# A recurrent-memory transformer on one core: the second turn of the probabilities as row-tile products in four banks, value groups and late outputs spread evenly over the steps, x as bf16 rows, dense weights loaded earlier

## The chip, the cores and the metric

The kernel runs on one core of a Trainium2 chip. The metric is the device time of one execution in microseconds (us); lower is better. Of the engines, TensorE (PE; its weight loads are shown apart as PEld) does the matrix products, VectorE (DVE) and ScalarE (ACT) read the results out of PSUM and do elementwise work, GpSimd (POOL) does elementwise work on SBUF, and SyncE (SP) issues most transfers.

## The reference

Four stages in a row on x (2048 rows of 512): attention with a recurrent memory, a dense block, the same attention again, the same dense block, each on a layer-normalized input and added to its residual.

```python
def _A_ref(x, mem0, Wq, Wk, Wv, Wo, seg_len):      # H = 32 heads of 128, M = 8, seg_len = 32
    mem = mem0
    for s in range(n_seg):                         # 64 segments
        h = concatenate([mem, x[segment s]])       # 8 + 32 = 40 rows
        q, k, v = h @ Wq, h @ Wk, h @ Wv           # per head
        p = softmax(mask(q @ k.T * scale))
        o = (p @ v) @ Wo                           # summed over heads
        mem = o[:8]
        outs.append(o[8:])
def _B_ref(x, w1, w2):                             # 512 -> 1376 -> 512
    return relu(x @ w1) @ w2
x = x + _A_ref(_layernorm(x), ...)
x = x + _B_ref(_layernorm(x), ...)
x = x + _A_ref(_layernorm(x), ...)
x = x + _B_ref(_layernorm(x), ...)
```

The memory makes attention sequential: segment s + 1 needs the memory that segment s left.

## The kernel before, in words

Everything is bf16 with f32 sums; all weights stay in SBUF. The program is one straight line of 67 steps (`step(k)`, k = 0 to 66; step 0 is `first_step`). Step k does segment k of the first attention layer (a = 0) and segment k - 3 of the second (a = 1) side by side, and between their parts the dense block for the segments that are ready. Steps 3 to 63 have both layers; the first three and the last three have one and are called single.

Inside a step with both layers the order on TensorE, VectorE, SP and GpSimd is the order of the source (`manual_schedule`); only ScalarE's order is left to the scheduler, which `evict_behind` steers: an eviction marked `late` is issued behind the last exponential. A step runs:

- `qk(0)`: queries and keys of heads 0 to 15 (tile `qp`, 128 products of 80 columns), then a piece of filler work, then `scores` into two banks that are kept for scores (`sp_banks`), `exponentials`, `softmax(0)`. The first half of the probabilities (`P_sb`) is turned by a transposing transfer (`turn_p`, on SP).
- `qk(1)`: the same for heads 16 to 31, then `dense_h` (tile `hp`), the second `scores`, `softmax(1)`. Its result `P1_sb` (in the profile it too is named P_sb) comes partly from GpSimd and, for a = 1, from VectorE.
- While the softmax runs on VectorE and ScalarE, TensorE has filler: value groups (`vp`), the values of the next segment of layer 1 (`v`), the late outputs (`wox`) and the second dense product (`dense_y`, written into a scores bank, so it shows as sp<-w_sb,hT).
- The second half is then turned on TensorE (`transpose_p(1, 5)`, tile `tp`, line 623): 16 products of a 128 x 64 block with the two-block identity, 80 columns each, in column tiles, into two banks of the pool `ps_c`: five slots copied out by ScalarE, three by VectorE, into `PT_sb`. The last 8 products of `dense_y` (from `f_mid = 9` on) stand between the turn and what follows.
- `weighted_v`: 64 products (`pv`), two row tiles of 40 rows at a time, heads in three groups of 12, 12 and 8, each with its bank; `outputs` copies them into `OTm` (memory rows) and `OTx` (token rows), VectorE for a = 0 and ScalarE for a = 1.
- `output_mem` (tile `wo`), `output_own` (`own`), the new memory (`mt`) and its values (`vm`); then `prepare(k + 1)`, which adds to the residual and normalizes.

PSUM has eight banks: `ps_c` three, `sp_banks` two, `ps_wo` one, `ps_fill` two.

What the change touches:

- `load_x` (lines 115 to 118): the rows of x of a segment go by two GpSimd transfers, which widen them to f32, into the residual tile; `add_own` (400 to 405) adds the attention's own output to it.
- `load_dense` (154 to 158): w1, then w2 in two parts; called in step 1 from `probabilities` (line 902). In step 0 the space of w1 and w2 serves as staging for values.
- `values_at` (739 to 748): which value groups (8 products each, the values of 64 tokens) are due in step k. From step 5 to step 61 the odd steps have one or two groups, the even ones none.
- `output_late` (379 to 385) and `add_late` (387 to 393): for a segment of layer 1 whose output does not ride with the memory output (every second one), 64 products in the step behind it, 20 of them ahead of the first scores (`first = 10` heads), into the bank of `ps_wo`, and two additions on VectorE ahead of the turn's copies. So odd steps have groups and no late outputs, even steps late outputs and no groups.

The steps in one table (k = 5 to 62):

| steps | value groups | late products | called below |
|---|---|---|---|
| even | 0 | 64 | even step |
| odd, 10 of 29 | 1 | 0 | one-group step |
| odd, 19 of 29 | 2 | 0 | two-group step |

Of the kernel before, what the change touches and what calls it, by code (L numbers as in the profile page):

```python
# [22 lines left out]
def kernel(  # L23
# [90 lines left out]

    def load_x(k):
# [38 lines left out]
    def load_dense():  # L154
        nc.sync.dma_start(out=w1_sb[:], in_=B_w1.rearrange("(c p) f -> p c f", p=128))
# [41 lines left out]
    P1_sb = const.tile([128, 16 * L + 24], BF)  # L197
# [110 lines left out]
    def values0(p, n, lo=0, hi=NC4, pool=None, stage=None, late=False):  # L308
        r = 64 * (p % 2)
        if (n, lo) == (0, 0):  # L310
            vd0[p] = dram.tile([4, 2, 64, 512], BF, tag="vd0", bufs=4, name="vd0")
# [54 lines left out]
    def output_rows(t, a, lo, hi):  # L366

        for h in range(lo, hi):
            for j in range(2):
                q = 32 * (2 * (h % 2) + j)  # L370
                nc.tensor.matmul(t[q:q + 32, 0:HALF], lhsT=OTx[:, h, SEG * a:SEG * a + SEG],  # L371
                                 rhs=Wo_sb[:, h, HALF * j:HALF * j + HALF], start=(h < 2), stop=(h >= H - 2),
                                 tile_position=(0, q))

    def late_rows(k):
        s = k - 1
        return s if has1(s) and not ride1(s) else None

    def output_late(k, lo, hi):
        if late_rows(k) is None:  # L380
            return
        if lo == 0:
            pool, tag = (ps_wo, "wo") if k <= LAST else (ps_c, "c")
            wo_tiles[k] = pool.tile([128, Dm], F32, tag=tag, name="wox")
        output_rows(wo_tiles[k], 1, lo, hi)

    def add_late(k, parts=range(2)):
        if late_rows(k) is None:
            return
        d, o = place1(late_rows(k))  # L390
# [9 lines left out]
    def add_own(k):  # L400
# [3 lines left out]
        for part in range(2):  # L404
            nc.vector.tensor_tensor(out=R, in0=R, in1=own_tiles[k][64 * part:64 * part + 64, 0:HALF], op=ALU.add)
# [194 lines left out]
    def softmax(hf, act, by_pe=False, ess=None):  # L600
        if ess is None:
            ess = exponentials(act)
        if by_pe and hf:
            transpose_p(0)
        for a, es in ess.items():
# [4 lines left out]
            P = P1_sb[:, 0:16 * L].rearrange("p (s a q) -> p s a q", s=8, a=2)[:, :, a, :] if hf else \  # L610
                P_sb[:, :, 64 * a:64 * a + L]
            eng.tensor_tensor(out=P, in0=es[:],  # L612
                              in1=sm[:].unsqueeze(2).to_broadcast([128, 8, L]), op=ALU.mult)

    def transpose_p(hf, cut=4):

        for s0, ns, copy in ((0, cut, nc.scalar.copy), (cut, 8 - cut, nc.vector.tensor_copy)):
            tp = ps_c.tile([128, ns, 2, L], F32, tag="c", name="tp")
            for sl in range(ns):
                for a in range(2):  # L620
                    c = L * (2 * (s0 + sl) + a)
# [435 lines left out]
```

## Time and profile before

| | |
|---|---|
| time before, median of 3 runs | 1618.14 us (1617.14 to 1618.94) |
| the profiled execution | 1617.83 us |
| its span in the profile | 1616.0 us, 103053 instructions |
| VectorE, ScalarE, GpSimd busy | 76%, 45%, 23% of the span |
| granted TensorE clock, mean | 0.998 |
| transfers | 146.25 MB, 91 GB/s on the mean |

How to read it: a row of the timeline has the start in us from the span's start, the duration, the engine, the line, the operation, output<-inputs, shapes and count; in brackets is the idle time of the engine just before, and what ended it. Successive instructions of one kind are merged (x24), and consecutive rows of an engine can overlap, since products and copies are pipelined: the time that a group takes from its engine is the difference of the starts of its row and the next. In a table of stretches the columns are the stretch, its length, busy time (and count) of PE, PEld, DVE, ACT and POOL, the granted clock, the transfer engines' share and GB/s. In rows of groups, the figure behind the busy time is the mean of one in ns.

### The profile page before, as it was taken

To read this page: it belongs to the slowest core of one execution; us is meant where nothing else is said; L and a number is where in the kernel's file an instruction comes from. 1 tells how busy PE (TensorE), PEld (TensorE's weight loads), DVE (VectorE), ACT (ScalarE), POOL (GpSimd) and SP (SyncE) were. 2 spreads that over 40 slices of the span, in tenths; PEclk is the share of its full clock that TensorE was granted. 3 is DMA by queue.
4 is the path that set the end of the run, shared out by engine and by line. 5 is a ranking of instruction groups with operands and counts; after the bars stand their busy time and mean duration, and the time that the engine had idled before them with its cause. 6 is when DMAs were issued, how large, how long until landed. Compare 5 with 4: busy or idle time off the path is not lost.

```text
span 1616.0 us, 103053 instructions
## 1 busy us (share of the span) xinstructions
PE 1568.8 (97%) x46705; PEld 1273.1 (79%) x46706; DVE 1229.6 (76%) x3463; ACT 728.4 (45%) x1708; POOL 365.4 (23%) x733
## 2 busy tenths in 40 slices
PE   6899999999999999999999999999999999999997
PEld 3578878888878877887888887788788878878875
DVE  4477878777877877887777787778777777877765
ACT  3344444444444444444444444444444444444442
POOL 2022222122222222212222222222222222222210
PEclk9999999999999999999999999999999999999999
DMA  9734343434344444443433444353443334335321
GB/s 367 217 90 78 84 75 86 88 74 87 76 85 82 84 89 70 93 76 77 90 83 87 72 84 82 71 96 79 81 83 76 83 70 90 79 74 86 74 66 38
DMA packets 226757, 146.25 MB, mean 91 GB/s; under 512 B 124392, under 2 KB 222736, under 8 KB 226320
## 3 DMA queue, kind: packets, MB, share of 16 engines
q1 hardware_dynamic: 220080, 135.44, 38.7%
q0 software_dynamic: 6144, 4.20, 1.8%
q8 instruction: 366, 6.00, 1.6%
q14 instruction: 71, 0.58, 0.1%
q10 hardware_dynamic: 96, 0.03, 0.0%
HBM read 65.41 MB, written 45.09 MB: 68 GB/s over the span
## 4 chain that ended last, share of the span: by engine, by line
PE 85%; DVE 3%; issue 2%; ACT 2%; POOL 0%; POOLq 0%; ACTq 0%
PE qp L539 36%; PE wo L581 7%; PE vm L724 7%; PE own L371 7%; PE hp L482 5%; PE v L357 5%; PE sp L498 4%; PE wox L371 4%; PE sp L573 3%; PE pv L649 3%; PE tp L623 2%; DVE es L595 1%; PE vp L318 1%; ACT es L597 1%; ACT vst L306 1%
## 5 line engine op out<-in xcount | busy, mean ns | idle before, releaser
L545 ACT CAST QT<-qp 128x480 bf16<-128x480 f32 (+3 forms) x402 | 200.3, 498 | 432.3 <-PE qp L539 430.1
L539 PE MATMUL qp<-HT,Wq_sb 128*128 128x80 bf16 (+1 forms) x8576 | 367.3, 200 | 1.8 <-POOL HT L710 1.2
L539 PEld LDWEIGHTS <-Wq_sb 128*128 128x128 bf16 x8576 | 323.1, 100 | 32.7 <-issue 27.0
L539 PE MATMUL qp<-HT,Wk_sb 128*128 128x80 bf16 (+1 forms) x8576 | 344.8, 200 | 1.9 <-issue 1.9
L539 PEld LDWEIGHTS <-Wk_sb 128*128 128x128 bf16 x8576 | 317.3, 100 | 2.8 <-issue 2.3
L612 POOL TENSOR_TENSOR P_sb<-es,sm 128x320 bf16<-128x320 f32 x186 | 131.6, 721 | 637.3 <-ACT es L597 476.2
L547 DVE CAST KT<-qp 128x480 bf16<-128x480 f32 (+3 forms) x402 | 220.2, 573 | 24.1 <-PE qp L539 20.8
L591 DVE TENSOR_REDUCE mx<-sp 128x8 f32<-128x320 f32 x256 | 114.4, 487 | 135.5 <-PE sp L573 135.5
L371 PEld LDWEIGHTS <-OTx 128*32 128x32 bf16 x6272 | 161.3, 96 | 26.0 <-issue 2.9
L357 PE MATMUL v<-Wv_sb,xnT 128*32 128x512 bf16 x2048 | 131.2, 380 | 2.8 <-ACT vst L306 1.1
L371 PE MATMUL own<-Wo_sb,OTx 128*32 128x256 bf16 x4096 | 131.5, 272 | 0.5 <-issue 0.3
L607 DVE TENSOR_REDUCE sm<-es 128x8 f32<-128x320 f32 x256 | 119.0, 465 | 14.9 <-ACT es L597 2.5
L597 ACT ACTIVATE es<-es 128x320 f32<-128x320 f32 x256 | 111.6, 468 | 38.8 <-DVE es L595 36.0
L581 PE MATMUL wo<-Wo_sb,OTm 128*32 128x512 bf16 x2112 | 127.7, 380 | 0.8 <-issue 0.8
L724 PE MATMUL vm<-Wv_sb,HTm 128*32 128x512 bf16 x2144 | 128.2, 379 | 0.1
L728 ACT CAST VmS<-vm 128x512 bf16<-128x512 f32 x132 | 77.2, 585 | 103.5 <-PE vm L724 103.5
L565 DVE CAST sp<-maskb 128x320 f32<-128x320 bf16 x256 | 118.6, 485 | 0.0
L595 DVE TENSOR_TENSOR es<-sp,mx 128x320 f32<-128x320 f32 x256 | 113.2, 482 | 0.5
L276 POOL TENSOR_TENSOR mv<-mv,mhalf_t 128x2 f32<-128x2 f32 (+1 forms) x66 | 46.5, 705 | 295.8 <-DVE mv L275 261.5
L498 PE MATMUL sp<-w_sb,hT 128*32 128x256 bf16 (+1 forms) x2772 | 104.8, 276 | 0.8 <-DMA w_sb<-in_B_w_dram 0.5
L482 PE MATMUL hp<-xnT,w_sb 128*128 128x64 bf16 (+1 forms) x2948 | 96.4, 192 | 5.5 <-DMA w_sb<-in_B_w_dram 5.1
L482 PEld LDWEIGHTS <-w_sb 128*128 128x128 bf16 x2948 | 90.3, 98 | 7.2 <-DMA w_sb<-in_B_w_dram 5.6
(122 smaller groups left out, 2052.4 us busy)
## 6 DMA issues: line engine op xcount, KB each, us to landing
Vs<-vd SPq DMA_DIRECT2D x96, 256.0 KB
vd<-vst SPq DMA_DIRECT2D x181, 128.0 KB
vmd<-VmS SPq DMA_DIRECT2D x132, 128.0 KB
Vs<-vmd SPq DMA_DIRECT2D x254, 32.0 KB
Vs<-vmd SPq DMA_DIRECT2D x60, 128.0 KB
Wq_sb<-in_A_Wq_dram SPq DMA_DIRECT2D x2, 2048.0 KB
Wk_sb<-in_A_Wk_dram SPq DMA_DIRECT2D x2, 2048.0 KB
Wv_sb<-in_A_Wv_dram SPq DMA_DIRECT2D x2, 2048.0 KB
```

Source lines behind the costliest of these rows:

```text
L357: nc.tensor.matmul(vp[32 * j:32 * j + 32, :], lhsT=tokens[c4], rhs=Wv_sb[:, c4, n * 512:(n + 1) * 512], start=(c4 == 0), stop=(c4 == NC4 - ...
L371: nc.tensor.matmul(t[q:q + 32, 0:HALF], lhsT=OTx[:, h, SEG * a:SEG * a + SEG], rhs=Wo_sb[:, h, HALF * j:HALF * j + HALF], start=(h < 2), s ...
L482: nc.tensor.matmul(hp[:, fc - f0, 0:n].rearrange("p (s t) -> p s t", s=ns), lhsT=w1_sb[:, c4, u:u + 128], rhs=cols(c4), start=(c4 == 0), s ...
L498: nc.tensor.matmul(sp_banks[1][32 * q:32 * q + 32, 0:w], lhsT=hT_tiles[d][0:fs, fc, SEG * o:SEG * o + SEG], rhs=w2_flat[0:fs, fc * Dm + HA ...
L539: nc.tensor.matmul(qp[:, hi, 0:ncol], lhsT=W_sb[:, c4, h * Dh:(h + 1) * Dh], rhs=HT[:, c4, a_lo:a_hi, :], start=(c4 == 0), stop=(c4 == NC4 ...
L545: nc.scalar.copy(out=dst[:, 0:nh, a_lo * L:a_hi * L], in_=qp[:, 0:nh, 0:ncol])
L547: nc.vector.tensor_copy(out=dst[:, 0:nh, a_lo * L:a_hi * L], in_=qp[:, 0:nh, 0:ncol])
L581: nc.tensor.matmul(wo[32 * j:32 * j + 32, :], lhsT=OTm[:, h, n, 2 * M * c:2 * M * c + 4 * M], rhs=Wo_sb[:, h, :], start=(h < 4), stop=(h > ...
L595: nc.vector.tensor_tensor(out=es[:], in0=sp, in1=mxs[a][:].unsqueeze(2).to_broadcast([128, 8, L]), op=ALU.subtract)
L597: last_exp[0] = nc.scalar.activation(out=es[:], in_=es[:], func=ACTF.Exp, scale=SCALE)
L612: eng.tensor_tensor(out=P, in0=es[:], in1=sm[:].unsqueeze(2).to_broadcast([128, 8, L]), op=ALU.mult)
L724: nc.tensor.matmul(vp[32 * j:32 * j + 32, :], lhsT=HTm[:, c4, :], rhs=Wv_sb[:, c4, n * 512:(n + 1) * 512], start=(c4 == 0), stop=(c4 == NC ...
```

## The change

The second turn becomes `turn_second`: `P1_sb` gets the layout of `P_sb` (eight slots of 128 columns, each layer's 40 at 0 or 64), and each of the 16 products now takes the 40 rows of one row tile (64 g) by all 128 columns of a slot against a 40-column identity. The four groups (u: slots 0 to 3 or 4 to 7; g: row tile) have a bank each, two of `ps_c` and two of `ps_fill`, and ScalarE and VectorE copy two each. All of `dense_y` stands ahead of it. In `weighted_v` the bank that lies in `sp_banks[0]` is that of the first head group instead of the second, and the third group takes `ps_fill`.

`values_at` gives one group to each of the steps 5 to 52 and none to the later ones. The late outputs are cut in two halves of 16 heads, one in the step behind the segment and one in the step after that (whole, as before, for the last segments); in steps with a value group they stand behind the second scores and take a bank of `ps_c`, since the value group has that of `ps_wo`. `add_late` runs in both steps. The value group's eviction is `late` now.

`load_x` brings the rows as bf16 into a tile of their own, on SP, and the first of the two additions of `add_own` reads that tile. `load_dense` is called in two parts, right behind the value loads of step 1 and behind its memory values.

```diff
     def load_x(k):
+        x_tiles[k] = wk.tile([64, HALF], BF, tag="x16", bufs=2, name="x16")
         for j in range(2):
-            nc.gpsimd.dma_start(out=residual(k)[SEG * j:SEG * j + SEG, :],
-                                in_=A_x[0, SEG * k:SEG * k + SEG, HALF * j:HALF * j + HALF])
+            nc.sync.dma_start(out=x_tiles[k][SEG * j:SEG * j + SEG, :],
+                              in_=A_x[0, SEG * k:SEG * k + SEG, HALF * j:HALF * j + HALF])
...
-    P1_sb = const.tile([128, 16 * L + 24], BF)
+    P1_sb = const.tile([128, 8, 128], BF)
...
+    def late_jobs(k):
+        jobs = []
+        for s in (k - 1, k - 2):
+            if has1(s) and not ride1(s):
+                parts = ((0, H // 2), (H // 2, H)) if s <= NSEG - 3 else ((0, H), (0, 0))
+                lo, hi = parts[k - 1 - s]
+                if hi > lo:
+                    jobs.append((s, lo, hi))
+        assert len(jobs) < 2
+        return jobs[0] if jobs else None
...
+        if lo == h0:
+            pool, tag = (ps_c, "c") if k > LAST or values_at(k) else (ps_wo, "wo")
...
-            nc.vector.tensor_tensor(out=R, in0=R, in1=own_tiles[k][64 * part:64 * part + 64, 0:HALF], op=ALU.add)
+            nc.vector.tensor_tensor(out=R, in0=R if part else x_tiles.pop(k)[:], in1=own_tiles[k][64 * part:64 * part + 64, 0:HALF],
+                                    op=ALU.add)
...
+    def turn_second():
+
+        tps = {}
+        for u in range(2):
+            for g in range(2):
+                pool, tag = (ps_fill, "fill") if u else (ps_c, "c")
+                tps[u, g] = pool.tile([128, 4, L], F32, tag=tag, name="tp")
+            for sl in range(4):
+                for g in range(2):
+                    R = 64 * g
+                    nc.tensor.matmul(tps[u, g][:, sl, :], lhsT=P1_sb[R:R + L, 4 * u + sl, :],
+                                     rhs=ident[R:R + L, R:R + L], start=True, stop=True)
+        for u in range(2):
+            for g, copy in ((0, nc.scalar.copy), (1, nc.vector.tensor_copy)):
+                copy(out=PT_sb[:, 4 * u:4 * u + 4, g, :], in_=tps[u, g][:])
...
-                if (t, a) == (1, 1):
+                if (t, a) == (0, 1):
...
-                    pool, tag = (ps_fill, "fill") if t + a == 1 else (ps_c, "c")
+                    pool, tag = (ps_fill, "fill") if t == 2 else (ps_c, "c")
...
-        if k % 2 == 0 or k > NSEG - 3:
-            return []
         groups = [(p, n) for p in range(9, NSEG // 2, 2) for n in range(0, NCH, 2)]
-        i, n = (k - 5) // 2, (NSEG - 6) // 2
-        return groups[len(groups) * i // n:len(groups) * (i + 1) // n]
+        return groups[k - 5:k - 4]
...
             if k == 1:
+                load_dense(0)
                 memory_values(k)
+                load_dense(1)
                 inputs_T(3)
-        first = 4 if k == LAST else 8 if single else 10
+        first = 4 if k == LAST else 8 if single else 0 if values_at(k) else 10
...
-        value_group(k, 0, 2, NC4)
+        value_group(k, 0, 2, NC4, late=True)
...
+        output_late(k, second, H)
         if has0(k) and has1(k + 1):
             values1(k + 1, 0)
-        output_late(k, second, H)
...
-            dense_y(d, 0, f_mid)
+            dense_y(d, 0, NFC)
...
-            transpose_p(1, 4 if single else 5)
-        if k < LAST:
-            dense_y(d, f_mid, NFC)
+            turn_second()
```

More of the change, by code (lines that the diff above doesn't have):

```diff
@@ L620, in transpose_p @@
+    def transpose_p():
+        for s0, copy in ((0, nc.scalar.copy), (4, nc.vector.tensor_copy)):
+            tp = ps_c.tile([128, 4, 2, L], F32, tag="c", name="tp")
+            for sl in range(4):
                 for a in range(2):
[L621 to L623 removed]
+                    nc.tensor.matmul(tp[64 * a:64 * a + 64, sl], lhsT=P_sb[:, s0 + sl, 64 * a:64 * a + 64], rhs=ident_q,
```

56 lines of the change are left out of this document (23 added, 33 removed).

## The prediction

> **What bounds the kernel now.** I read the page first (busy shares, chain of waits), then the timeline of TensorE over three successive steps, then VectorE and ScalarE around the second softmax, and last the start.
>
> ```profile
> PE 1568.8 (97%) x46705; PEld 1273.1 (79%) x46706; DVE 1229.6 (76%) x3463; ACT 728.4 (45%) x1708; POOL 365.4 (23%) x733
> PE 85%; DVE 3%; issue 2%; ACT 2%; POOL 0%; POOLq 0%; ACTq 0%
> ```
>
> TensorE is busy for 97% of the span and holds 85% of the chain that ended last: what shortens its stream shortens the kernel, unless a wait takes the place.
>
> ```profile
> 764.66 1.03 PE L539 MATMUL qp<-HT,Wq_sb 128*128 128x80 bf16 x24
> ...
> 788.56 1.03 PE L539 MATMUL qp<-HT,Wq_sb 128*128 128x80 bf16 x24
> ...
> 800.39 0.58 PE L573 MATMUL sp<-KT,QT 128*40 128x40 bf16 x32
> ...
> 803.84 1.18 PE L498 MATMUL sp<-w_sb,hT 128*32 128x320 bf16 x36
> 804.98 0.48 PE L623 MATMUL tp<-ident,P_sb 128*64 128x80 bf16 x16
> 805.39 0.40 PE L498 MATMUL sp<-w_sb,hT 128*32 128x256 bf16 x8
> 805.73 0.49 PE L649 MATMUL pv<-PT,Vs 40*128 40x40 bf16 x25
> ...
> 806.63 1.91 PE L581 MATMUL wo<-Wo_sb,OTm 128*32 128x512 bf16 x32
> 808.37 1.05 PE L371 MATMUL own<-Wo_sb,OTx 128*32 128x256 bf16 x32
> 809.24 0.26 PE L767 MATMUL mt<-sel,wm 128*32 128x16 bf16 x16
> ...
> 812.10 1.03 PE L539 MATMUL qp<-HT,Wq_sb 128*128 128x80 bf16 x24
> ...
> 823.76 0.57 PE L573 MATMUL sp<-KT,QT 128*40 128x40 bf16 x32
> 824.18 0.60 PE L318 MATMUL vp<-Wv_sb,xT 128*64 128x512 bf16 x4
> 824.72 1.91 PE L357 MATMUL v<-Wv_sb,xnT 128*32 128x512 bf16 x32
> 826.45 1.18 PE L498 MATMUL sp<-w_sb,hT 128*32 128x320 bf16 x36
> 828.12 0.48 PE L623 MATMUL tp<-ident,P_sb 128*64 128x80 bf16 x16 [0.49 <-DVE mv L219]
> ...
> 835.24 0.93 PE L539 MATMUL qp<-HT,Wq_sb 128*128 128x80 bf16 x21
> ```
>
> A step runs from one first query product (qp, x24) to the next. The two-group step takes 788.56 - 764.66 = 23.90 us, the even step with its 64 late products (wox) 812.10 - 788.56 = 23.54, the one-group step 835.24 - 812.10 = 23.14. I cut a step in three: to the second scores (sp x32), 800.39 - 788.56 = 11.83 even and 823.76 - 812.10 = 11.66 odd; from there to the memory output (wo), 806.63 - 800.39 = 6.24 even; and the rest, 812.10 - 806.63 = 5.47. The change works on the middle part. Only the one-group step shows a wait there, 0.49 before the turn (tp), and what it waits for stands on VectorE (the three rows of 802 and the two of 804 are from the even step, whose second scores began at 800.39):
>
> ```profile
> 824.18 0.89 DVE L591 TENSOR_REDUCE mx<-sp 128x8 f32<-128x320 f32 x2 [1.26 <-PE sp L573]
> ...
> 827.35 0.62 DVE L612 TENSOR_TENSOR P_sb<-es,sm 128x320 bf16<-128x320 f32 x1
> 827.90 0.17 DVE L219 BATCH_NORM_AGGREGATE mv<-stats 128x2 f32<-128x6 f32 x1
> 828.10 0.15 DVE L220 TENSOR_SCALAR mv<-mv 128x1 f32<-128x1 f32 x1
> ```
> ```profile
> 802.13 0.47 ACT L597 ACTIVATE es<-es 128x320 f32<-128x320 f32 x1 [1.03 <-DVE es L595]
> 802.51 0.57 ACT L306 CAST vst<-v 128x512 bf16<-128x512 f32 x1
> 802.97 0.47 ACT L597 ACTIVATE es<-es 128x320 f32<-128x320 f32 x1
> ```
> ```profile
> 804.87 0.88 DVE L393 TENSOR_TENSOR R<-R,wox 64x256 f32<-64x256 f32 x2
> ...
> 805.77 0.41 DVE L627 CAST PT_sb<-tp 128x240 bf16<-128x240 f32 x1
> ```
>
> In that step P1 is written at 827.35 + 0.62 = 827.97, 4.21 after the second scores began, and the turn starts 0.15 later. In the even step the two additions of the late outputs (804.87, 0.88 for both) stand between P1 and VectorE's copy of the turned tile; P1 comes by 804.87 there, 4.48 after the scores, an eviction of 0.57 (vst) having stood between ScalarE's two exponentials.
>
> **The change, part by part.**
>
> *Turn.* It took 805.39 - 804.98 = 0.41, and the 8 dense products behind it 805.73 - 805.39 = 0.34, a change of tile shape in each. Afterwards all 44 dense products stand ahead of it: the 36 took 804.98 - 803.84 = 1.14, and 8 more at the rate of the own products (809.24 - 808.37 = 0.87 for 32) add 0.22, so 1.36. The trace has no turn of 40 rows by 128 columns, but the weighted values (pv) have this form and shape, and 64 of them take 806.63 - 805.73 = 0.90, 0.014 each with the change of shape at their end. The bounds are 0.13 (half of the 80 columns, at the late products' 0.027 for 256 columns in four tiles, 0.0085 each) and today's 0.41. I take 0.21 for 16, being the same form. TensorE's own stream is shorter by 0.41 + 0.34 - 0.22 - 0.21 = 0.32 a step.
>
> *Copies.* Two become four, of 160 columns; the nearest rows are those of that width:
>
> ```profile
> L545 ACT CAST QT<-qp 128x160 bf16<-128x160 f32 x12 | 3.5, 292 | 13.3 <-PE qp L539 13.3
> L547 DVE CAST KT<-qp 128x160 bf16<-128x160 f32 x12 | 3.8, 317 | 0.1
> L623 PE MATMUL tp<-ident,P_sb 128*64 128x80 bf16 x1120 | 33.6, 203 | 8.0 <-DVE P_sb L612 4.8 <-DVE mv L219 2.4 <-POOL HT L710 0.5
> ```
>
> So 0.29 on ScalarE and 0.32 on VectorE, twice each, where VectorE had one of 0.41. Today 8 dense products and 32 weighted values of the first half cover them; afterwards only the latter, and the banks are shared with them. Without that cover the first copy would stand bare, about 0.20 (a product's latency, the last row) + 0.32.
>
> *Value group and late outputs.* The products are the same in number (64 late outputs in two halves of 32, one group of 8 a step instead of none, one or two): no work is removed, steps become equal. Where a group is due, the middle part without stalls is: scores 0.42 (824.18 - 823.76), half group 0.54 (824.72 - 824.18), 32 late products 0.87, values 1.73 (826.45 - 824.72), dense 1.36, turn 0.21, weighted values 0.90 (806.63 - 805.73), together 6.03. The turn is reached at 0.42 + 0.54 + 0.87 + 1.73 + 1.36 = 4.92, behind P1 at 4.21: the 0.49 wait is gone.
>
> What is late next: VectorE has the additions in every step now, 4.24 to 5.12, and its two copies queue behind them. TensorE leaves the turn at 5.13; the first weighted values take the late outputs' bank (the third of three in that pool), free at about 5.17. 24 products (0.30) later, at 5.47, it needs the banks of the first two copies: a product's latency after 5.02 puts ScalarE's at 5.51 and VectorE's at 5.54, with 0.05 for the hand-over 5.59 (an estimate: VectorE passed from the additions to the copy in 0.02, P1 to the turn took 0.15). 24 more to 5.89, then the second copies (5.86, so 5.91), then the rest, 0.30: memory output at 6.21, and I take 6.20. Stalls 0.17, of a possible 0 to 0.44 (twice a bare copy's 0.52 less the 24 products' 0.30). The step is 11.66 + 6.20 + 5.47 = 23.33.
>
> Today's 48 steps 5 to 52 are 24 even, 9 one-group and 15 two-group: (24 x 23.54 + 9 x 23.14 + 15 x 23.90) / 48 = 23.58. Gain 48 x 0.25 = 12.0. In 11 of them (k % 4 == 1 with an x tile to come) the statistics' tail (827.90 to 828.25, 0.35) also stands between the additions and the copies; the copies end 0.35 later and 0.25 of that shows: -2.8. Net 9.2.
>
> Steps 53 to 62 have no group. There the middle part comes to the turn early (0.42 + 0.33 for 12 late products + 1.73 + 1.36 = 3.84) and waits for P1 as the one-group step did, to 4.36; VectorE's copies end at 5.44 and 5.76, the memory output starts at about 6.11, and the step is 11.83 + 6.11 + 5.47 = 23.41 against (5 x 23.54 + 23.14 + 4 x 23.90) / 10 = 23.64: 2.3. Step 4 and the steps of one layer at both ends: 1.1 as an estimate (at most 0.32 for each of seven).
>
> *x as rows.* Two POOL transfers a step become two on SP, ahead of the values' writes. SP is empty there:
>
> ```profile
> 799.20 1.24 SPq L630 DMA_TRANSPOSE PT<-P_sb  x1
> 803.10 0.36 SPq L362 DMA_DIRECT2D vd<-vst  x1
> ```
>
> Between the turn of P (over at 800.44) and the first write 2.66 us are free, and two issues of this kind (0.36 for the write) fit in; behind them wait only the value writes and the output rows. The tile comes 20 us before its use. The first addition now reads it as bf16, at the same length. I take nothing; if that cover were gone, 0.7 a step on SP, which nothing on the chain sees. On POOL the weights for the softmax are not behind a transfer now; no chain link is POOL's, so nothing again.
>
> *Dense weights.*
>
> ```profile
> 69.72 1.36 PE L482 MATMUL hp<-xnT,w_sb 128*128 128x32 bf16 x44 [5.13 <-DMA w_sb<-in_B_w_dram]
> ...
> 73.43 1.19 PE L498 MATMUL sp<-w_sb,hT 128*32 128x320 bf16 x18 [0.51 <-DMA w_sb<-in_B_w_dram]
> ```
> ```profile
> 56.26 0.33 SPq L694 DMA_DIRECT2D Vs<-vd_second  x1
> ...
> 61.77 0.41 SPq L155 DMA_DIRECT2D w_sb<-in_B_w_dram  x1
> ```
> ```profile
> 65.00:68.00 3.00, 0.00 (x0) 0.00 (x0) 0.92 (x3) 0.20 (x1) 0.00 (x0) 1.00 1.04 401
> 68.00:71.00 3.00, 1.28 (x44) 1.25 (x44) 0.00 (x0) 0.25 (x1) 0.00 (x0) 0.75 1.07 357
> 71.00:74.00 3.00, 2.49 (x22) 1.19 (x21) 0.00 (x0) 0.97 (x2) 0.00 (x0) 0.68 0.34 109
> ```
>
> Step 1 loses 5.13 + 0.51 waiting for weights issued from 61.77, and after the long wait the granted clock is 0.75 and 0.68 for two stretches of 3 us: at 0.68, 71 to 74 loses 0.96. With the issue behind the row at 56.26 the first matrix leaves SP some 5 us earlier. But the second now stands ahead of the transposed rows the same products read, four x transfers more stand ahead on SP, and the transfer engines are full (401 GB/s). Bounds: 0 and 5.64 + 0.96 = 6.6. I take 4.5, 3.5 of the waits and the 0.96 (2.1 of wait left), nearer the upper bound, since the first matrix can leave SP as much earlier as TensorE waited.
>
> [...]
>
> **Sum.** 9.2 + 2.3 + 1.1 + 4.5 = 17.1. The profiled run took 1617.83, 0.31 below the median shown; 1618.14 - 17.1 = 1601.0.
>
> **The rivals.**
>
> *Copies take it all.* The stall is 0.44 rather than 0.17: 58 x 0.27 = 15.7 of the gain are gone, leaving 1.4, or 1616.7. For it: four copies, each with a bank that the next product needs. Against: 24 products (0.30) still lie between. [...]
>
> *VectorE is the new bound: slower.* P1 comes late in every step, because an eviction (0.57) stands before an exponential: 4.21 + 0.57 = 4.78; then the additions and two copies, 4.78 + 0.03 + 0.88 + 0.64 + 0.05 + 0.30 = 6.68. It decides from P1 at 4.55, where the middle part reaches 23.58 - 11.66 - 5.47 = 6.45. Price: 11.66 + 6.68 + 5.47 = 23.81, 0.23 over 23.58, in 58 steps 13.3; less the start's 4.5 and 1.1 it is 1618.14 + 7.7 = 1625.8. For it: in the even step an eviction there made P1 4.48. Against: in the changed order the evictions stand behind both exponentials.
>
> *No stall at all, start bare.* 48 x (23.58 - 23.16) + 2.3 + 7 x 0.32 + 6.6 = 31.3: 1586.8. For it: VectorE's consecutive copies overlap by some 0.09 in its rows (two mx of 487 ns in 0.89). Against: the bank of the late outputs is busy to 5.12.
>
> *The start does not change* (the second matrix and the rows behind it just take the wait over): 1605.5, the rest as forecast.
>
> **How the numbers follow.** Forecast 0.57, start unchanged 0.08, copies take it all 0.13, VectorE the bound 0.10, no stall 0.12. The range 1586 to 1617 leaves out the slow case and what lies beyond the good one; the forecast's own is 1593 to 1609 (stalls 0.14 more or less). 0.2% is 3.2 us, about what a measurement of this kernel can tell from no change: faster is below 1614.9, slower above 1621.4. A third of the copies' case counts as faster: 0.57 + 0.08 + 0.12 + 0.04 = 0.81; same 0.09; slower 0.10.
>
> **What would show it.** Steps 5 to 52 all near 23.33 (23.58 in 11 of them); 16 turn products in about 0.21; TensorE idle before pv by waits on the two copies, not before tp; steps 53 to 62 waiting about 0.4 for P1; the hp wait in step 1 near 2 us and clock 1.00 behind it. Wrong it would be if the middle part exceeds 6.45, if P1 comes after 4.55, or if the first dense product still starts near 69.7.

## The result, and the profile after

| | before | changed kernel |
|---|---|---|
| median of four runs each | 1617.79 us | 1600.91 us (1599.17 to 1603.53) |
| ratio, 95% interval | | 0.9896 (0.9879 to 0.9914) |
| profiled execution, span | 1617.83, 1616.0 | 1602.42, 1600.5 |
| granted clock, mean | 0.998 | 0.996 |
| VectorE, GpSimd busy | 76%, 23% | 79%, 19% |

The kernel became 1.0% faster, and 1600.91 us is almost the 1601.0 forecast. The terms behind it are another matter. I cut both profiled spans at TensorE's first product (4.6 us in, in both), at the first query product (qp) of step 2 and of each later step, as the prediction did, and at the last output transfer:

| part | before | after | difference | forecast |
|---|---|---|---|---|
| steps 0 and 1 | 77.07 | 79.25 | +2.18 | -4.5 |
| steps 2 to 4 | 66.34 | 65.13 | -1.21 | with the two rows marked "ends": -1.1 |
| steps 5 to 52 | 1138.21 | 1125.46 | -12.75 | -9.2 |
| steps 53 to 62 | 237.08 | 234.29 | -2.79 | -2.3 |
| step 63 | 23.37 | 25.38 | +2.01 | ends |
| steps 64 to 66, to the last output transfer | 63.27 | 63.53 | +0.26 | ends |
| from there to the end of the span | 6.08 | 2.89 | -3.19 | 0 |
| sum | | | -15.49 | -17.1 |

**The steady steps.** TensorE's timeline of the changed kernel: one step with a value group (a group step) in detail, and the starts of the three behind it, of which the second (from 805.02) carries the statistics' tail (the same columns as before):

```profile
758.46 1.03 PE L556 MATMUL qp<-HT,Wq_sb 128*128 128x80 bf16 x24
...
770.08 0.57 PE L590 MATMUL sp<-KT,QT 128*40 128x40 bf16 x32
770.49 0.60 PE L323 MATMUL vp<-Wv_sb,xT 128*64 128x512 bf16 x4
771.02 1.06 PE L376 MATMUL wox<-Wo_sb,OTx 128*32 128x256 bf16 x32
771.91 1.90 PE L362 MATMUL v<-Wv_sb,xnT 128*32 128x512 bf16 x32
773.63 1.40 PE L515 MATMUL sp<-w_sb,hT 128*32 128x320 bf16 x44
774.97 0.37 PE L641 MATMUL tp<-ident,P_sb 40*128 40x40 bf16 x16
775.24 0.18 PE L677 MATMUL pv<-PT,Vs 40*128 40x40 bf16 x1
...
775.78 0.56 PE L677 MATMUL pv<-PT_sb,Vs 40*128 40x40 bf16 x32
776.27 1.91 PE L598 MATMUL wo<-Wo_sb,OTm 128*32 128x512 bf16 x32
...
781.74 1.03 PE L556 MATMUL qp<-HT,Wq_sb 128*128 128x80 bf16 x24
...
805.02 1.03 PE L556 MATMUL qp<-HT,Wq_sb 128*128 128x80 bf16 x24
...
828.62 1.03 PE L556 MATMUL qp<-HT,Wq_sb 128*128 128x80 bf16 x24
```

The step takes 781.74 - 758.46 = 23.28, the one with the tail 828.62 - 805.02 = 23.60. The first part is 770.08 - 758.46 = 11.62, the middle part 776.27 - 770.08 = 6.19 and the rest 5.47. Every step from 5 to 52 is now of one of these two kinds. The turn takes 775.24 - 774.97 = 0.27, and nothing waits ahead of it. The 64 weighted values take 776.27 - 775.24 = 1.03, where they took 0.90 in the kernel before: 0.09 more in the first half and 0.04 in the second, which I put down to the banks of the copies. VectorE in the same step:

```profile
773.66 0.62 DVE L628 TENSOR_TENSOR P_sb<-es,sm 128x320 bf16<-128x320 f32 x1
774.31 0.88 DVE L409 TENSOR_TENSOR R<-R,wox 64x256 f32<-64x256 f32 x2
775.31 0.56 DVE L645 CAST PT_sb<-tp 128x160 bf16<-128x160 f32 x2
```

P1 is written at 774.28, 4.20 after the second scores began; the additions and both copies of the turned tile follow without a hole to speak of, and end at 775.87.

The waits of TensorE that belong to the turn over the whole span (us in total, times, longest):

```profile
PE pv L677 <- DVE PT_sb L645: 6.5, 25, 0.4
...
PE tp L641 <- DVE P_sb L628: 3.0, 8, 0.4
```

Of the 25 waits on VectorE's copy, 11 stand in the steps with the tail and one in each of the steps 53 to 62; in a plain group step the stall is too short for the profile to list. In each of the steps 53 to 62 TensorE also waits 0.38 before the turn; the profile names P1 there in six steps, and in four a small copy on GpSimd.

**The start.** TensorE and SP of the changed kernel in step 1, and the granted clock there (the column of 1.00, 0.51 and so on):

```profile
65.52 0.22 PE L590 MATMUL sp<-KT,QT 128*40 128x40 bf16 x3 [2.12 <-issue]
...
72.24 1.34 PE L499 MATMUL hp<-xnT,w_sb 128*128 128x32 bf16 x44 [3.75 <-DMA x<-in_A_x_dram]
```
```profile
49.83 0.90 SPq L120 DMA_DIRECT2D x<-in_A_x_dram  x2
...
57.38 0.33 SPq L722 DMA_DIRECT2D Vs<-vd_second  x1
57.77 0.44 SPq L159 DMA_DIRECT2D w_sb<-in_B_w_dram  x1
...
62.82 3.17 SPq L297 DMA_TRANSPOSE xnT<-XN  x1
```
```profile
63.00:66.00 3.00, 0.88 (x34) 0.69 (x35) 0.38 (x2) 0.07 (x2) 0.23 (x2) 1.00 1.07 378
66.00:69.00 3.00, 2.49 (x15) 1.00 (x9) 2.34 (x6) 1.78 (x4) 0.00 (x0) 0.51 1.63 295
69.00:72.00 3.00, 0.00 (x0) 0.00 (x0) 0.00 (x0) 0.11 (x1) 0.00 (x0) 0.50 0.56 129
72.00:75.00 3.00, 2.76 (x52) 1.76 (x51) 0.00 (x0) 0.63 (x2) 0.00 (x0) 0.50 0.01 3
75.00:78.00 3.00, 3.00 (x62) 2.01 (x61) 0.54 (x3) 1.07 (x3) 0.00 (x0) 0.79 0.12 44
```

The first weight matrix does leave SP 4 us earlier (57.77 instead of 61.77), and the dense products no longer wait for it. They begin later all the same, at 72.24 instead of 69.72. Their other input, the transposed rows (xnT), leaves SP at 62.82 (58.3 before), behind both matrices, and keeps SP for 3.17. The profile puts the wait down to an x transfer, which these products don't read; in n_add, t_tail and q_early below the same wait has the name of the transposed rows. Before it, TensorE loses 2.12 amid the scores to nothing that the profile names. The clock is at half for 10.2 us in all (twice 3 x (0.49 + 0.50 + 0.50 + 0.21)), where before it was 3.4.

**The end.** The last output transfer and the span, after and then before, and the queue that exists only before:

```profile
1597.61 0.78 SPq L1043 DMA_DIRECT2D out_dram<-ob  x2
```
```profile
span 1600.5 us, 103205 instructions
```
```profile
1609.92 0.78 SPq L1021 DMA_DIRECT2D out_dram<-ob  x2
```
```profile
span 1616.0 us, 103053 instructions
...
q0 software_dynamic: 6144, 4.20, 1.8%
```

The same transfers stand 2.89 from the end after and 6.08 before. In that time the trace of before has SP done with its part of the closing at 1612.1 and the first closing instruction of GpSimd only at 1615.3; after, only 0.03 lie between the two. GpSimd's queue of 6144 packets, the x rows, is gone.

**Step 63.** One stretch at half clock, 3.41 us from 1526.94, with TensorE idle for 0.91 in the 3.41 us before it:

```profile
1527.00:1530.00 3.00, 3.00 (x32) 1.11 (x36) 1.94 (x6) 0.87 (x4) 0.79 (x2) 0.50 0.00 0
```
```profile
1526.92 3.58 PE L598 MATMUL wo<-Wo_sb,OTm 128*32 128x512 bf16 x32
```

The memory output there takes 3.58 instead of 1.91. In s_old, q_early and q_best it takes 1.91 in that step, and the trace of before has half clock only from 69.51 to 72.93 in step 1 and again from 1612.34, behind the last output transfer.

### The profile page after: what moved, and what is told of

The parts are those of the page before. It is cut to its first block, busy times and chain, and to the rows that moved or that the text cites. A ratio compares the mean times of both kernels' runs of the same rounds, so it can differ in the third digit from the quotient of the medians.

```text
span 1600.5 us, 103205 instructions
## 1 busy us (share of the span) xinstructions
PE 1557.3 (97%) x46705; PEld 1273.2 (80%) x46706; DVE 1259.8 (79%) x3590; ACT 727.2 (45%) x1775; POOL 298.5 (19%) x605
## 4 chain that ended last, share of the span: by engine, by line
PE 87%; DVE 6%; DMA 2%; issue 2%; ACT 1%; SPq 1%; POOL 0%; ACTq 0%; POOLq 0%
PE qp L556 37%; PE wo L598 8%; PE vm L752 7%; PE own L376 7%; PE hp L499 5%; PE v L362 4%; PE sp L590 3%; PE pv L677 3%; PE vp L323 3%; PE sp L515 3%; PE wox L376 3%; DMA Wv_sb<-in_A_Wv_dram 2%; DVE sm L624 1%; DVE R L409 1%; DVE P_sb L628 1%
## 5 line engine op out<-in xcount | busy, mean ns | idle before, releaser
L376 PEld LDWEIGHTS <-OTx 128*32 128x32 bf16 x6272 | 155.2, 96 | 41.2 <-issue 22.7
L362 PE MATMUL v<-Wv_sb,xnT 128*32 128x512 bf16 x2048 | 121.8, 379 | 0.0
L515 PE MATMUL sp<-w_sb,hT 128*32 128x256 bf16 (+1 forms) x2772 | 93.0, 276 | 0.3
```

The source lines that it names most:

```text
L362: nc.tensor.matmul(vp[32 * j:32 * j + 32, :], lhsT=tokens[c4], rhs=Wv_sb[:, c4, n * 512:(n + 1) * 512], start=(c4 == 0), stop=(c4 == NC4 - ...
L515: nc.tensor.matmul(sp_banks[1][32 * q:32 * q + 32, 0:w], lhsT=hT_tiles[d][0:fs, fc, SEG * o:SEG * o + SEG], rhs=w2_flat[0:fs, fc * Dm + HA ...
```

## The experiments

The experiments ran on other chips, where the kernel before took 1621.8 to 1622.9 us (median of each batch). So times are compared as ratios to the kernel before on the same chip, and parts by the steps of the profiled executions. No trace of the kernel before from those chips is on record, so a sum over many steps, set against the first chip's trace, can hold a few us that aren't the edit's. The commonest step doesn't move with the chip: p_x has the 23.54 and 23.90 of the kernel before, and every kernel with both the spreading and the new turn has 23.28. And steps 0 and 1 vary from execution to execution: n_add, t_tail and the changed kernel have the same instructions there and took 78.09, 81.27 and 79.25. So one pair of kernels can't settle less than about 3 us in the start. All results in one table (us; a group step without and with the statistics' tail, medians over steps 5 to 52; for kernels with the old filler these are mixed and left out; "close" is from the last output transfer to the end of the span):

| kernel | ratio (95%) | steps 0+1 | group step / with tail | steps 53 to 62 | close |
|---|---|---|---|---|---|
| before | 1 | 77.07 | | 237.08 | 6.08 |
| changed | 0.9896 (0.9879 to 0.9914) | 79.25 | 23.28 / 23.60 | 234.29 | 2.89 |
| p_spread | 0.9903 (0.9877 to 0.9930) | 77.08 | 23.48 / 23.42 | 233.32 | 6.05 |
| p_turn | 0.9976 (0.9961 to 0.9991) | 78.12 | | 238.11 | 6.11 |
| p_x | 0.9992 (0.9973 to 1.0011) | 79.26 | | 238.35 | 2.88 |
| n_add | one run, 1598.59 us | 78.09 | 23.28 / 23.59 | 231.57 | 2.94 |
| t_tail | 0.9868 (0.9853 to 0.9883) | 81.27 | 23.28 / 23.29 | 234.55 | 2.92 |
| s_old | 0.9887 (0.9871 to 0.9904) | 78.81 | 23.31 / 23.59 | 234.57 | 3.47 |
| s_split | 0.9902 (0.9883 to 0.9921) | 79.17 | 23.28 / 23.60 | 234.95 | 2.92 |
| s_split_tail | 0.9877 (0.9862 to 0.9892) | 82.22 | 23.28 / 23.30 | 234.08 | 3.03 |
| q_old | 0.9871 (0.9851 to 0.9891) | 76.74 | 23.29 / 23.59 | 234.63 | 2.96 |
| q_early | 0.9863 (0.9839 to 0.9887) | 75.07 | 23.28 / 23.59 | 234.76 | 2.98 |
| q_best | 0.9856 (0.9839 to 0.9874) | 76.12 | 23.28 / 23.28 | 234.50 | 3.76 |
| q_early_tail | 0.9850 (0.9836 to 0.9864) | 76.53 | 23.28 / 23.28 | 235.05 | 3.78 |

### Where the steady gain comes from

**p_spread: the kernel before with only value groups and late outputs spread** (values_at, late_jobs, output_late and add_late as in the change, and six buffers instead of four for the values in DRAM, which the change has too; the old turn).

```diff
-        first = 4 if k == LAST else 8 if single else 10
+        first = 4 if k == LAST else 8 if single else 0 if values_at(k) else 10
...
-        if k % 2 == 0 or k > NSEG - 3:
-            return []
...
-        i, n = (k - 5) // 2, (NSEG - 6) // 2
-        return groups[len(groups) * i // n:len(groups) * (i + 1) // n]
+        return groups[k - 5:k - 4]
```

> The kernel before with the late outputs in two halves and one value group a step alone; turn, x and dense weights as before. Theory A: steps 5 to 52 take 11.66 + 6.35 + 5.47 = 23.48 (23.58 on the mean before), steps 53 to 62 about 23.3 (23.64), together 8 us, time 1609 to 1611. Rival B: as no work is removed, nothing changes: 1617 to 1619. If the gains of the two parts simply add, this and the turn alone make 11 to 14 us, less than the 15 to 17 seen in the steps; if they help each other (the spread hides the additions), the sum stays short of it.

Two successive steps of it:

```profile
760.22 1.03 PE L550 MATMUL qp<-HT,Wq_sb 128*128 128x80 bf16 x24
...
783.69 1.03 PE L550 MATMUL qp<-HT,Wq_sb 128*128 128x80 bf16 x24
...
807.25 1.03 PE L550 MATMUL qp<-HT,Wq_sb 128*128 128x80 bf16 x24
```

Group steps of 23.47 and 23.56 here, 23.48 in the median. Spreading alone takes 7.1 us from steps 5 to 52 (1131.14) and 3.8 from 53 to 62, together 10.9 and more than the 8 expected, and its ratio is 0.9903, not to be told from the changed kernel's 0.9896: it carries most of the steady gain.

**p_turn: the kernel before with only the new turn** (turn_second and the new banks of weighted_v).

```diff
-            transpose_p(1, 4 if single else 5)
-        if k < LAST:
-            dense_y(d, f_mid, NFC)
+            turn_second()
...
```

> The kernel before with the new turn alone (row tiles, four banks, all dense products ahead of it, the banks of the weighted values as changed); groups, late outputs, x and dense weights as before. Theory A (TensorE's stream is 0.32 us shorter a step, but VectorE's additions stand ahead of its two copies): even steps 23.54 to 23.7 (no gain: the additions end 5.36 after the second scores began), two-group steps 23.90 to 23.75, one-group steps 23.14 to 22.8; 3 to 6 us in all, time 1612 to 1615. Rival B (only TensorE's stream counts): every step 0.32 shorter, 60 steps, 19 us, time 1599. Rival C (four copies cost more than they give): even steps 23.8 or more, time above 1618.

```profile
765.36 1.03 PE L539 MATMUL qp<-HT,Wq_sb 128*128 128x80 bf16 x24
...
789.13 1.03 PE L539 MATMUL qp<-HT,Wq_sb 128*128 128x80 bf16 x24
...
812.99 1.03 PE L539 MATMUL qp<-HT,Wq_sb 128*128 128x80 bf16 x24
```

The two-group step falls from 23.90 to 23.77, and 22.78 is the median of the one-group steps (23.14 before); the even step with its 64 late products is longer (23.86 here, 23.65 the commonest, 23.83 in the median, 23.54 before). VectorE's additions still stand there ahead of the copies, which no product covers any more: this kernel waits 5.0 us, in 29 waits, for VectorE's copy before the weighted values, in nearly all of the even steps and hardly any other. By the commonest steps (15, 9 and 24 of them) that is -2.0 - 3.2 + 2.6 = -2.6 us; the sum over steps 5 to 52 (1137.55) is only 0.7 below that of the kernel before, since single hold-ups cost 1.9 more in it, and the ratio is just under 1. Taken on top of the spreading the turn is worth more: steps 5 to 52 go from 1131.14 to 1125.46, but 53 to 62 lose 1.0. And with the new turn the tail shows: with the old one the steps that carry it are no longer than the others (23.42 and 23.48), with the new one 0.32 longer. So the parts don't simply add up.

**n_add: the changed kernel without the additions of late outputs in steps 53 to 62** (those rows of the output lack the attention's own output).

```diff
-            add_late(k)
+            if not 53 <= k <= 62:
+                add_late(k)
```

> The changed kernel without the additions of the late outputs in steps 53 to 62 (left out, so ten segments' outputs lack a part). If VectorE's additions (0.87 us) ahead of its copies set the pace of these steps, they fall from 23.41 to about 22.9 us, 4.8 us in all; if P1 or the copies themselves do, they stay at 23.4.

```profile
1298.06 1.03 PE L556 MATMUL qp<-HT,Wq_sb 128*128 128x80 bf16 x24
...
1321.00 1.03 PE L556 MATMUL qp<-HT,Wq_sb 128*128 128x80 bf16 x24
```

The step takes 22.94, 0.47 less than the 23.41 of the changed kernel, and so do the four other even steps. The wait for VectorE's copy before the weighted values, 0.28 to 0.36 in the changed kernel, is gone from all ten. So in steps without a group the copies' place behind VectorE's 0.88 of additions sets the pace, as the prediction's step for them has it. The five odd steps, though, are at 23.08 to 23.61, so that the ten together gave 2.7 us (231.57) and not the 4.8 expected; what held the odd ones stays open.

**t_tail: the changed kernel with the statistics' tail behind the output copies.**

```diff
-        elif not single and k % 4 == 1 and has_x:
-            mom["x"] = stat_tail(mom["stats"])
...
             outputs(k, pvs)
+        if not single and k % 4 == 1 and has_x:
+            mom["x"] = stat_tail(mom["stats"])
```

> The changed kernel with the tail of the x statistics (two short VectorE operations in 11 steps, k = 5 to 45) moved from ahead of VectorE's copies of the turned tile to behind the copies of the outputs. If VectorE's queue ahead of those copies sets the start of the weighted values, these 11 steps fall from 23.59 to 23.28 us, 3.4 us in all, time 1597.5. Rival: if ScalarE's copies or the turn itself set it, the steps stay at 23.59 and the time at 1600.9.

```profile
PE hp L499 <- DMA xnT<-XN: 9.0, 1, 9.0
```

The steps with the tail fall from 23.60 to 23.29, those without stay, and the wait for VectorE's copy is gone from all 11: the tail's place on VectorE was the whole 0.31, and 0.31 x 11 = 3.4 us are to be had. In step 1, which has no such tail, this execution waited 9.0 for the transposed rows (named so here) and lost 2 us more than the changed kernel; the ratio is better nevertheless, though the two intervals just touch (0.9883 and 0.9879).

### Why the start got longer

**s_old: the changed kernel with the dense weights at their old place in step 1.**

```diff
-                load_dense(0)
                 memory_values(k)
-                load_dense(1)
...
                 load_x(k + 1)
+            if k == 1:
+                load_dense(0)
+                load_dense(1)
```

> The changed kernel with both parts of the dense weights loaded where they were before (behind the first half's softmax of step 1). Theory A: in the changed kernel the transposed rows that the first dense products read were issued behind both weights (at 62.82 us) and came in behind them, so that the early load cost time; undone, the first dense product starts near 70 (72.24 changed, 69.72 before), the 2.12 us hole in the scores of step 1 goes, the granted clock is low for about 3.4 us instead of 10.2, steps 0 and 1 together take 77.1 to 77.6 us (79.26 changed, 77.07 before), and the time is 1597 to 1599. Rival B: the early load did its work and something else in the start is slower (the x transfers on SP): then steps 0 and 1 together take more than 79.3 and the time is above 1602.

```profile
71.52 1.35 PE L499 MATMUL hp<-xnT,w_sb 128*128 128x32 bf16 x44 [6.96 <-DMA w_sb<-in_B_w_dram]
```

Steps 0 and 1 stay at 78.81, 1.7 above the kernel before, with the weights loaded exactly where it loads them: between the two ranges expected, so that neither theory is met. The wait for the transposed rows is gone, one of 6.96 for the weights stands in its place. So something else of the change seems to lengthen the start.

**s_split and s_split_tail: only the first matrix early, the second at the old place** (the second kernel with t_tail's move as well).

```diff
                 load_dense(0)
                 memory_values(k)
-                load_dense(1)
...
                 load_x(k + 1)
+            if k == 1:
+                load_dense(1)
```

> The changed kernel with the first dense weight loaded early as it is and the second where it was before, so that the transposed rows stand ahead of the second weight on SP. Theory A (the rows queue behind the weights): rows in by 64 to 66, first dense product at 64.7 to 67, no low clock or at most one stretch of 3.4 us, steps 0 and 1 together 71 to 74 us, time 1592 to 1595. Rival B (the first weight itself is what comes late, the transfer engines being full): first dense product still at 70 or later, steps 0 and 1 together above 77, time 1598 or more.

> Both of the last two edits together. If they are independent their gains add: steps 0 and 1 together 71 to 74 us and 11 steps at 23.28, time 1588.5 to 1591.5. If the start's gain is only a shift of waits: 1597 or more.

```profile
68.21 0.50 PE L499 MATMUL hp<-xnT,w_sb 128*128 128x32 bf16 x12
...
74.47 2.59 PE L515 MATMUL sp<-w_sb,hT 128*32 128x320 bf16 x22 [3.11 <-DMA w_sb<-in_B_w_dram]
```

The first dense products start at 68.21 without a wait, and the second ones wait 3.11 for their matrix, which now left SP only at 67.76; in s_split_tail it is 5.57. Steps 0 and 1 take 79.17 and 82.22: the wait moved, nothing was won, and neither theory is met whole. It does show that the transposed rows were late for standing behind the second matrix: sent ahead of it, they cost 0 and 0.72. In s_split_tail the commonest step with the tail is 23.28, as in t_tail.

**p_x: the kernel before with only the x rows on SP as bf16.**

```diff
-            nc.gpsimd.dma_start(out=residual(k)[SEG * j:SEG * j + SEG, :],
+            nc.sync.dma_start(out=x_tiles[k][SEG * j:SEG * j + SEG, :],
...
```

> The kernel before with x as bf16 rows on SP alone. Theory A: nothing on the chain waits for these transfers, every step as before, time within 2 us of 1617.8. Rival B: the four more transfers at the start delay the staging writes and with them the dense weights: steps 0 and 1 together 78 to 80 instead of 77.1, time 1618.5 to 1621. Rival C: GpSimd's weights, freed of 0.54 us transfers, come sooner and steps shorten: below 1615.

```profile
62.74 2.28 SPq L120 DMA_DIRECT2D x<-in_A_x_dram  x2
65.07 0.42 SPq L158 DMA_DIRECT2D w_sb<-in_B_w_dram  x1
```

This edit alone gives the longer start. The rows of the next segment hold SP for 2.28 right ahead of the weights, which leave at 65.07 instead of 61.77; the dense products begin at 71.21 instead of 69.72, and the row of the 18 second dense products takes 1.75 (from 75.06) instead of 1.19. Steps 0 and 1 take 79.26, 2.2 over the kernel before (and over p_spread, which leaves the x rows where they were). At the other end the closing falls from 6.08 to 2.88, so that the whole, 0.9992, shows nothing. That the close goes with GpSimd's queue is seen in every row of the table: the three kernels that bring all x rows through it have 6.05 to 6.11, all others 2.88 to 3.78.

**q_old, q_early, q_best and q_early_tail: the x rows of the first segments (k up to 3) on GpSimd's queue, all others on SP,** with the dense weights at the old place, early, at the old place with t_tail's move, and early with that move.

```diff
-            nc.sync.dma_start(out=x_tiles[k][SEG * j:SEG * j + SEG, :],
+            (nc.gpsimd if k <= 3 else nc.sync).dma_start(out=x_tiles[k][SEG * j:SEG * j + SEG, :],
```

> The changed kernel with the dense weights at their old place in step 1, and the x rows of segments 1 to 3 (steps 0 to 2) on POOL's queue instead of SP's, as bf16 rows; the other x rows stay on SP. Theory A (the start got longer because the x transfers on SP push the weights and the transposed rows behind them): steps 0 and 1 together fall from 78.8 us (weights at the old place, x on SP) to the 77.1 that the kernel before has; group steps stay at 23.28 and 23.60; ratio to before about 0.988. Rival B (the turn or the new copies lengthen the single steps, x is innocent): steps 0 and 1 stay at 78.5 or more.

> The changed kernel, dense weights early as in the change, x rows of segments 1 to 3 on POOL's queue. Theory A (the weights ahead of the transposed rows hold those rows back, whoever carries x): hp still waits for the transposed rows until about 71 to 72 us and steps 0 and 1 together stay at 78.5 to 79.3. Rival B (it was the x transfers alone that undid the early load): the first hp product starts before 69, steps 0 and 1 together are 74 to 76.5, and the prediction's 4.5 us comes at least by half.

> Three things together: dense weights at the old place, x rows of segments 1 to 3 on POOL's queue, and the statistics' tail behind the copies of the outputs. If the parts add up: steps 0 and 1 together 77.1 us, group steps 23.28 in all of the steps 5 to 52 (also in the 11 with the tail), 53 to 62 at 23.41, and a time about 5 us below the changed kernel: ratio to before about 0.986. If the start is a matter of chance and not of the queue, steps 0 and 1 stay between 78.5 and 81, ratio 0.988.

> The changed kernel (dense weights early) with the x rows of segments 1 to 3 on POOL's queue and the statistics' tail behind the copies of the outputs. If the parts add up: steps 0 and 1 together 75.1 us as without the tail moved, hp waits about 2.8 us and starts by 69, all of the steps 5 to 52 at 23.28, ratio to before about 0.985 (0.983 to 0.987). Rival (the moved tail brings the wait for the transposed rows back, as it did with x on SP): hp waits 4 us or more for xnT, steps 0 and 1 together 77 to 81, ratio 0.986 to 0.988.

TensorE, SP and the clock in q_early:

```profile
68.42 1.34 PE L499 MATMUL hp<-xnT,w_sb 128*128 128x32 bf16 x44 [2.77 <-DMA xnT<-XN]
69.69 1.92 PE L323 MATMUL vp<-Wv_sb,xT 128*64 128x512 bf16 x8
71.54 1.48 PE L515 MATMUL sp<-w_sb,hT 128*32 128x320 bf16 x22
```
```profile
55.12 0.48 SPq L159 DMA_DIRECT2D w_sb<-in_B_w_dram  x1
...
61.25 1.68 SPq L297 DMA_TRANSPOSE xnT<-XN  x1
```
```profile
66.00:69.00 3.00, 0.57 (x22) 0.57 (x22) 0.84 (x3) 0.64 (x3) 0.00 (x0) 0.89 0.96 175
69.00:72.00 3.00, 3.00 (x45) 1.53 (x43) 0.00 (x0) 0.93 (x3) 0.00 (x0) 0.54 0.03 9
```

Segment 0's rows are among them, so it is eight small transfers, six of which fall in steps 0 and 1. With these off SP, the start is shorter. In q_early SP reaches the weights at 55.12 instead of 57.77, the transposed rows leave at 61.25 instead of 62.82 and keep it for 1.68 instead of 3.17, the dense products begin at 68.42 with a wait of 2.77, and no wait for the second matrix follows. Steps 0 and 1 take 75.07, 4.2 less than in the changed kernel and 2.0 less than before. Over all fourteen traces, the seven with these x rows on SP have 78.09 to 82.22 for steps 0 and 1 (median 79.25), the seven without 75.07 to 78.12 (76.74): the x rows were the loss, some 2.5 us. What the early weights are worth by themselves isn't shown: 1.7 by q_early against q_old (76.74), but -0.4 by q_early_tail against q_best, which in steps 0 and 1 have the same source as that pair. Against the kernel before at most 2.0 of the 4.5 forecast came, so q_early's Rival B is met in the start and not in the gain; q_old's Theory A is met.

The tail's move keeps its 0.31 a step in q_best and q_early_tail. The start of q_early_tail is not as good as q_early's, with the same source there:

```profile
PE sp L590 <- issue: 2.0, 1, 2.0
PE hp L499 <- DMA xnT<-XN: 1.9, 1, 1.9
```

The hole amid the scores is there again, 2.0, as in the changed kernel. It doesn't add to the time by itself, since the wait for the rows behind it is that much shorter (1.9); but the rows let the dense products begin only at 69.97, 1.55 later than in q_early, and the clock was at half for 6.8 us (0.55, 0.50 and 0.81 in the stretches 66 to 69, 69 to 72 and 72 to 75). The start is 1.5 longer. q_best and q_early_tail have the lowest ratios, 0.9856 and 0.9850; by their intervals q_early, q_old and t_tail can't be told from them. The intervals of q_best (up to 0.9874) and q_early_tail (up to 0.9864) lie below that of the changed kernel (from 0.9879), though on different chips.

## Why the prediction was right, point by point

The time was right to 0.1 us. That is partly chance. The start was wrong by 6.7 us; the steps 5 to 62 gained 4.0 more than forecast and the end 3.2 that I had not looked at, step 63 lost 2.0, and the pair of profiled executions differs by 15.4 where the medians differ by 16.9.

- *Turn.* 0.27 for the 16 products instead of 0.21, the whole middle part 6.19 instead of 6.20, a group step 23.28 instead of 23.33, with the tail 23.60 instead of 23.58. P1 came 4.20 after the scores (4.21 forecast, and 4.55 the limit set). Right.
- *Copies.* Stalls 0.13 in the weighted values and 0.06 in the turn (0.27, and 0.20 in n_add's steps of 22.94), 0.19 instead of 0.17. Neither "copies take it all" nor "no stall" came. n_add and t_tail show directly that work on VectorE ahead of the copies is what TensorE feels: 0.47 and 0.31 a step came back when it was taken away or moved.
- *Steps 5 to 52.* At 23.28 in 37 steps and 23.60 in 11 the sum is 1121.0 against 48 x 23.58 = 1131.8 by the steps of before, a gain of 10.8 where 9.2 was forecast, a group step being 0.05 shorter than forecast. The measured 12.75 has 1.9 more, because single hold-ups cost 6.4 over those sums before and 4.5 after. Of these, 2.4 and 0.8 are holes of over 0.2 us without a named releaser (the last section has more on them); the cause of the rest stays open. The forecast has no term for this 1.9, so that it came is luck.
- *Steps 53 to 62.* 23.41, as forecast, and the wait before the turn is 0.38 in each (about 0.4 forecast).
- *x as rows: "I take nothing".* This is the step that failed, twice. I looked at SP in a steady step, where 2.66 us are free, and the change there does cost nothing: p_x's commonest steps are those of the kernel before. In steps 0 and 1 SP is issuing almost without a break from 37 to 68 us: p_x puts the price at 2.2 us alone, the two groups of seven traces at 2.5, q_early against the changed kernel at 4.2. And the queue that x left, GpSimd's, had a price at the end of the program, 3.2 us, which stood in the page of before as 6.1 us between the last transfer and the end of the span.
- *Dense weights: 4.5.* In the change as it is, nothing of it came. With the x transfers away it came to 2.0 against the kernel before in q_early, and to 0.5 in q_early_tail. In q_early the waits fell by 2.9 (5.13 + 0.51 less 2.77) where 3.5 was forecast, with the wait left at 2.77 (2.1 forecast), but the dense products began only 1.3 earlier (68.42 against 69.72), since TensorE also came to them later; the 0.96 of the clock did not come, since the clock fell in q_early too (0.89 and 0.54 in the rows shown). The forecast took the whole 0.96 back with a wait of 2.1 still left; no run shows that, and q_early has 3.4 us at half clock behind its 2.77, as long as the kernel before has behind its 5.13. In the changed kernel what I had named as the danger, the second matrix ahead of the transposed rows with x transfers ahead of both, took the wait over: the rival "the start does not change", and worse by 2.2.
- *The ends.* -1.2 in steps 2 to 4 and +0.3 in 64 to 66, together near the -1.1 forecast, but +2.0 in step 63 from the half clock, whose cause stays open.

The clock remains. In q_early a wait of 2.77 is followed by a stretch at half clock, 2 x 3 x (0.11 + 0.46) = 3.4 us by the two clock rows shown for it. The stretches inside the program last 3.41 us in the kernel before (from 69.51), 10.24 and 3.41 in the changed kernel (from 66.04 and 1526.94), 3.4 in q_early and 6.8 in q_early_tail: one, two or three times 3.41. The two of the changed kernel begin 428 times 3.413 apart, and the one of before begins 452 times 3.413 ahead of the fall at 1612.34. The time without a product just ahead of a fall was not the same: of the 3.41 us before it, 3.41 in the kernel before, 2.49 in the start of the changed kernel and 0.91 in its step 63. And 1.52 of 3.41 us (before, 62.69 to 66.10) and 1.33 (changed kernel, 1588.38 to 1591.80) were followed by full clock. What decides when the clock falls isn't settled by this.

## What to carry to other kernels

Price a moved transfer in every phase of the program in which it runs, not in the steady state alone: a queue that has room in 60 steps can be the bound of the first two (SP here, with 2.66 us free in a steady step and almost no break from 37 to 68 us). Look at what stands between the last useful instruction and the end of the span; leaving a queue shortened it by 3.2 us here. Where a part of the program varies by 3 us from execution to execution, compare groups of traces, not pairs. And when a fixed amount of filler hides a serial chain, spreading it equally was worth more here than making the chain's own operations faster (0.9903 against 0.9976), but what stands ahead of the chain's copies on their engine comes through to the time: 0.31 of the tail's 0.35, and 0.47 of the additions' 0.88.

## What the runs showed of the hardware

- The three kernels that send x rows through GpSimd's queue all the way (6144 packets of software_dynamic in the page of before) close 6.05 to 6.11 us behind their last output transfer, those that use that queue for eight transfers or none 2.88 to 3.78. What GpSimd does in the 3.2 us the trace doesn't name.
- Half clock came in stretches of 3.41 us (before, changed kernel), 6.8 (q_early_tail) and 10.24 (changed kernel). One of 3.41 came in step 63 of the changed kernel with TensorE idle for only 0.67 and 0.24 in the 3 us before; the step took 25.38 us there and 23.37 before.
- From 50 us on to 20 us before the end, TensorE has seven holes of over 0.2 us without a named releaser in the trace of before and four in that of the changed kernel. Each of the eleven ends 1.3 to 1.5 us after a packet (16 KB) of a queue that the profile calls instruction has come in, where 5% of all moments lie so. In six traces such a hole stands amid step 1's scores, behind the 13th of the 16 products: 2.12 us in the changed kernel, 1.8 in s_split, 1.6 in s_split_tail, 2.0 in q_early_tail, 0.7 in n_add, 0.3 in p_x. A full share of the transfer engines doesn't go with it each time: it is 1.07 at 63 to 66 in the changed kernel and 1.11 in q_early, which has none there. What causes these holes, no run tested. The row of that queue in the changed kernel (packets, MB, share of 16 engines):

```profile
q8 instruction: 366, 6.00, 1.6%
```
